# When VectorE takes sums of attention's weights ahead of mixing steps: a change to a scheduled BigBird and FNet kernel

## The chip, the cores and the metric

The kernel runs on one core of a Trainium2 chip. Its time is the device time of one launch in microseconds, a median of three runs. One further launch was recorded by the profiler; every stretch of time below is from that one.

## The reference

Two blocks follow each other. The first is attention with BigBird's block mask (4 batches, 8 heads, 768 positions, 64 channels a head); the second mixes by Fourier transforms, normalises, and runs a small network over the channels.

```python
scores = scale * np.matmul(q, k.transpose(0, 1, 3, 2))
scores = np.where(mask, scores, -1000000000.0)          # mask: blocks of 32
attn = np.exp(scores - np.max(scores, axis=-1, keepdims=True))
attn = attn / (np.sum(attn, axis=-1, keepdims=True) + 1e-09)
out = np.matmul(attn, v)
x = out.transpose(0, 2, 1, 3).reshape(B, S, H * D)      # 4 x 768 x 512
X = np.fft.fft(np.fft.fft(x, axis=1), axis=2)
u = x + np.real(X)
un = (u - mean(u)) / np.sqrt(var(u) + 1e-06)            # over the 512 channels
return u + np.maximum(un @ w_ch1, 0.0) @ w_ch2          # 512 -> 2048 -> 512
```

## The kernel before

Attention works on pairs of heads, n = 0 to 15, four pairs to a batch. A pair has twelve units, u = 12 n + w. A unit is 128 keys against one half (384) of the queries, for both heads: TensorE makes its scores s (L592, and L602 where the mask is added by TensorE too), ScalarE the exponential into e (L612; or L620 and then a multiplication by the mask on VectorE, L622), TensorE the product with the values (L666). The six units of a half are also added up, element by element, in an accumulator acc: that is `gather(u)`. A sum is one instruction on VectorE (L647, 128 x 768) or two on GpSimd (L652, 128 x 384 each). TensorE then adds acc over its partitions into sp (L751; `total`), VectorE puts sp away in sums (L719 for the first pair of a batch, L721 for the others), and the pair's outputs are transposed into xt (L689) and copied into x (L690). There are four buffers of e and two of acc; scores have two banks of PSUM, and sp and xt share one, ps_t.

Mixing runs beside the attention of the next batch. VectorE folds the rows of x by their symmetries (L802 to L846), TensorE transforms (zp, L874, and the transform across channels), VectorE adds the result to x (L944), takes means and variances (L955, L956, with GpSimd in L957 and L959), normalises (L969) and transposes blocks of 32 (L1031). Two groups of DMAs turn these: far from un, then unT from far (L1047). `right` (L1092) makes combinations of unT, `left` (L1105, L1106 for a fold; L1112) combinations of the first weights.

The first product of the channels is Strassen's (Winograd's form) on quads of tiles: `quad(p)` issues seven products on TensorE (L1138), adds them on VectorE (L1143) and applies relu on ScalarE (L1147). Inside it, `combine(j)` prepares the next quad's left operand on VectorE: j = 1 is the fold and is two instructions, j = 3 is one. The second product comes in one of two forms. Where `seven[p // 2]` is set, two quads make a round with seven products (yc, yz, yw, L1246); its right operands wt and of come from GpSimd (L1215, `round_right`), its left ones are prepared on GpSimd or VectorE (L1228, L1231), and ScalarE, VectorE and GpSimd add what comes out (L1251 to L1290). Elsewhere `channels` makes plain products y (L1305) that VectorE adds to x (L1310).

Everything is emitted by one planner in Python. It keeps a clock per engine (`when`); `busy(engine, cost, after)` moves one on. Each engine runs its instructions in the order in which the planner emitted them. The planner looks into four queues (`short`, `apart`, `late`, `due`) and puts steps of mixing between the steps of attention. `do_apart` takes one step of mixing; its kind is a letter: d, w and b are steps that are VectorE's, m and t need a bank of PSUM, "-" needs none. For kind b, the right combinations after the blocks have gone through DRAM, `state["back"]` is the time from which unT may be read, by an estimate, BACK[b], added to the clock.

For a unit whose mask TensorE adds, the sum is not emitted at once. The unit waits in `to_gather` and its sum is emitted when its products with the values are, or when a later step asks for it (`gather_to`). `gather` picks the engine by the planner's clocks:

```python
at = max(e_at[u], acc_at.get((n, half), 0.0))
sooner = max(when["DVE"], at) + 1.0 < max(when["POOL"], at) + 2.9
```

Of the kernel before, what the change touches and what calls it, by code (L numbers as in the profile page):

```python
# [104 lines left out]
def kernel(  # L105
# [93 lines left out]
    when = {"PE": 0.0, "ACT": 0.0, "DVE": 0.0, "POOL": 0.0}  # L199
    free = {"m": [0.0, 0.0], "t": [0.0]}  # L200

    def busy(engine, us, after=0.0):
        when[engine] = max(when[engine], after) + us
        return when[engine]
# [8 lines left out]
    def give(which, at):  # L213
        free[which[0]][which[1]] = at + HOP
# [3 lines left out]
    def room(i, shape, name, dtype=FP32):  # L218
        return big.tile(shape, dtype, tag=f"big{i}", name=name)
# [281 lines left out]
    by_pe, to_gather = set(), deque()  # L501
# [3 lines left out]
    s_at, e_at, e_free, oT_at, acc_at = {}, {}, {}, {}, {}  # L505
# [127 lines left out]
    def gather(u):  # L633


        n, w = divmod(u, UP)
        half, c = divmod(w, C)
        if c == 0:
            return
        if c == 1:  # L640
            acc_of[n, half] = acc_p.tile([P, 2, HS], FP32, tag="acc", name="acc")
        acc, e = acc_of[n, half], e_of[u]
        start = e_of[u - 1] if c == 1 else acc
        at = max(e_at[u], acc_at.get((n, half), 0.0))
        sooner = max(when["DVE"], at) + 1.0 < max(when["POOL"], at) + 2.9
        if u in by_pe and masks["by_pe"] and w < UP - SLOT and sooner:
            nc.vector.tensor_tensor(out=acc, in0=start, in1=e, op=ALU.add)  # L647
            acc_at[n, half] = busy("DVE", 1.0, at) + HOP
        else:

            for i in range(2):
                nc.gpsimd.tensor_add(out=acc[:, i, :], in0=start[:, i, :], in1=e[:, i, :])  # L652
            acc_at[n, half] = busy("POOL", 2.9, at) + HOP
        e_free[u] = acc_at[n, half]
# [344 lines left out]
    def mixer(b, xA, xB):  # L999
# [57 lines left out]
        def un_back():  # L1057
# [5 lines left out]
            fetch(1)  # L1063
            state["back"] = max(when["PE"], state["ready"]) + BACK[b] + late_by

# [51 lines left out]
        def quad(p):  # L1117

            g = p // 2 % 2 if last else 0
            if p % 2 == 0:  # L1120
                for i in range(2):
                    hs[g, i] = room((2, 0)[g] + i, [P, 4, HS], "h" + "AB"[i])
            if not last:
                if p % 2 == 0:
                    seven[p // 2] = state["alone"] and p // 2 < NF // 4 - 1
                elif seven[p // 2]:
                    state["drain"]()
                    sums_room()
                    for j in (1, 2, 4, 3):
                        round_right(p // 2, j)  # L1130
            l1, l2 = 2 * (p % 2), 2 * (p % 2) + 1
            h11, h12, h21, h22 = (hs[g, i][:, l, :] for l in (l1, l2) for i in range(2))
            a11, a12, s2, a22 = blocks(p)
            b11, b21, b22 = unT[0][:, K1, :], unT[0][:, K2, :], unT[1][:, K2, :]

            def product(to, a, c, after=0.0):
                for k in range(ND // 2):
                    nc.tensor.matmul(to, a[:, k, :], c[:, k, :], start=(k == 0),  # L1138
                                     stop=(k == ND // 2 - 1))
                return busy("PE", PRODUCT, after) + HOP  # L1140

            def plus(to, ps, a, at):
                tt(out=to, in0=ps, in1=a, op=ALU.add)  # L1143
                return busy("DVE", SUM, at) + HOP

            def relu(h, at):
                nc.scalar.activation(out=h, in_=h, func=ACT.Relu)  # L1147
                busy("ACT", RELU, at)

            def combine(j):  # L1150
                left(p + 1, j)
                busy("DVE", COMBINE)

            x, at = ps_m.tile([P, 512], FP32, tag="m", name="xp")[:, 0:HS], bank("m")
            z5, z7 = (ps_s.tile([P, 2, 512], FP32, tag="s", name=name)[:, 0, 0:HS]
                      for name in ("z5", "z7"))
            done = product(x, a11, b11)
            nc.scalar.copy(out=h11, in_=x)  # L1158
            p1 = busy("ACT", RELU, done) + HOP
            give(at, p1 - HOP)  # L1160
            y, at = ps_m.tile([P, 512], FP32, tag="m", name="yp")[:, 0:HS], bank("m")
            p2 = product(y, a12, b21)
            done = product(z7, s2, t[2])
            u2 = plus(h21, z7, h11, max(done, p1))
            c11 = plus(h11, y, h11, p2)
            relu(h11, c11)
            done = product(z5, s[1], t[1])
            plus(h12, z5, h21, done)
            combine(1)
            done = product(z7, s[3], t[3], u2)  # L1170
            u3 = plus(h21, z7, h21, done)
            c22 = plus(h22, z5, h21, done)
            z_at[0] = c22
            relu(h22, c22)
            combine(3)
            gap(0.0, 1.9)
            done = product(y, a22, t[4], c11)
            c21 = plus(h21, y, h21, done)
            give(at, c21 - HOP)
            relu(h21, c21)  # L1180
            gap(0.0, 1.9, "t")
            done = product(z7, s[4], b22, u3)
            z_at[1] = plus(h12, z7, h12, done)
            relu(h12, z_at[1])
            combine(4)
            if last:
                for j in ((1, 2), (3, 4))[p % 2]:
                    output_right(p // 4, j, p // 2 % 2)
            elif p % 2 == 1 and seven[p // 2]:
                state["soon"] = 0.4  # L1190

        seven = {}
# [161 lines left out]
        last = b == B - 1  # L1354
# [139 lines left out]
        for r in range(0 if last else NF // 4):  # L1494
# [9 lines left out]
    MOST, LEAST = 9.6, 2.5  # L1504
    COVER = 100.0
    AHEAD = 2.2
    BACK = 11.0, 13, 11.5
    HALF = 5.0
    ALONE = 3.0
    LEAVES = 13.0  # L1510
# [6 lines left out]
    state = {"paired": False, "total": None, "w": 0, "got": 0, "owed": 0.0, "ready": 0.0,  # L1517
             "back": 0.0, "place": None,
             "slot": 0, "alone": False, "drain": lambda: None}
# [5 lines left out]
    def behind(kind):  # L1525

        at = max(when["DVE"], state["ready"])
        return (0.25 if state["alone"] else 0.75) * (len(kind) - 1) if when["POOL"] > at else 0.0

    def do_apart():  # L1530
        kind, fn, pe, act, dve, _ = apart.popleft()
        if finished and kind[0] in "mt" and state["total"] in short:
            short.remove(state["total"])
            state["total"][2]()
        if kind[0] in "dwb":
            dve += behind(kind)
            state["ready"] = busy("DVE", dve, {"w": rstd_at[0] if rstd_at else 0.0,
                                               "b": state["back"]}.get(kind, state["ready"])) + HOP
            fn()
            return  # L1540
        done = state["ready"]
        if kind != "-":
            at = bank(kind[0])
            done = busy("PE", pe, done) + HOP
        fn()
        if act:
            done = busy("ACT", act, done) + HOP
        if dve:
            done = busy("DVE", dve, done) + HOP
        if kind != "-":  # L1550
            give(at, done - HOP)
        state["ready"] = done
# [8 lines left out]
    def gap(rest=0.0, ahead=None, kinds="tm", start=None):  # L1561

        used = "".join(k for k in "tm" if k not in kinds)
        if ahead is None:
            ahead = AHEAD if late else ALONE
        while apart:
            kind, fn, pe, act, dve, need = apart[0]
            if len(late) > need:
                break
            if kind[0] in "dwb":  # L1570
                dve += behind(kind)
                if kind in "wb" and (state["back"] if kind == "b" else rstd_at[0]) > max(
                        when["DVE"], when["PE"]) + 0.2:
                    break
                at = max(when["DVE"], state["ready"]) - when["PE"]
                if at + dve > rest + ahead if start is None else at > start:
                    break
            elif kind != "-":
                bank_at = max(min(free[k]) for k in kind)
                if (any(k in used for k in kind) or  # L1580
                        max(state["ready"], bank_at) > when["PE"] + 0.1):
                    break
                used += kind
            do_apart()
        for item in list(short):
            kind, ready, fn = item
            if kind not in used and max(ready, min(free[kind])) <= when["PE"] + 0.1:
                used += kind
                short.remove(item)
                fn()  # L1590
# [334 lines left out]
```

## Time and profile before

| | |
|---|---|
| median of three runs | 1026.3 us (1026.03 to 1027.15) |
| the profiled execution | 1026.41 us |
| its span | 1024.7 us |
| TensorE's granted clock | 0.999 |
| VectorE, ScalarE, GpSimd busy | 712.2, 372.4, 326.7 us |
| sums on VectorE, mean of one | L647: 0.95 us where GpSimd rests beside it |
| half sums on GpSimd (L652) | 160 that add to acc, mean 1050 ns; 42 that start one, mean 1126 ns |

The span runs from the first instruction to the last; the profiled execution's own time is a little longer than it. A row of the timeline gives start and duration in us, the engine, the line, the operation, what it writes and reads, the count of instructions joined in it, and in brackets how long the engine had been idle and what it waited for. PE is TensorE, DVE VectorE, ACT ScalarE, POOL GpSimd, and SPq the queue that issues DMAs.

### The profile page before, as it was taken

What the parts mean: (1) busy time and instruction counts of PE and PEld (TensorE: products, weight loads), DVE (VectorE), ACT (ScalarE), POOL (GpSimd) and SP (SyncE); (2) the same over time, 40 slices, a digit from 0 to 9 for tenths busy, and PEclk for the clock granted to TensorE, in tenths of its full rate; (3) what the DMA queues carried; (4) which work ended last, traced back from release to release, by engine and by line L of the source; (5) the groups of instructions that cost most, each with busy time, mean ns of one, the idle gap of its engine ahead of it and who ended that gap; (6) DMA issues with size and microseconds to landing.
All of it is one profiled execution on the core that took longest, in us unless ns stands there. A gap on an engine that the chain in (4) does not pass through costs nothing.

```text
span 1024.7 us, 13026 instructions
## 1 busy us (share of the span) xinstructions
PE 1006.3 (98%) x4512; PEld 559.2 (55%) x4512; DVE 712.2 (70%) x1295; ACT 372.4 (36%) x763; POOL 326.7 (32%) x363
## 2 busy tenths in 40 slices
PE   8999999999999999999999999999999999999997
PEld 4344345444767764444444775444444765578576
DVE  6899895977984766755578577765458565775664
ACT  6888765553222222433440322343220221210210
POOL 1000173657634315454553232356450231000000
PEclk9999999999999999999999999999999999999999
DMA  7768422291000008532230002831010001200001
GB/s 228 228 190 231 102 48 47 52 150 31 1 1 1 11 11 151 96 73 39 55 62 1 1 11 77 155 58 41 17 24 8 1 0 52 42 1 0 1 13 52
DMA packets 182308, 60.44 MB, mean 59 GB/s; under 512 B 163018, under 2 KB 173012, under 8 KB 182236
## 3 DMA queue, kind: packets, MB, share of 16 engines
q1 hardware_dynamic: 180844, 58.88, 25.7%
q10 hardware_dynamic: 1360, 0.66, 0.3%
q8 instruction: 37, 0.61, 0.3%
q14 instruction: 35, 0.29, 0.1%
q0 software_dynamic: 32, 0.01, 0.0%
HBM read 46.14 MB, written 15.73 MB: 60 GB/s over the span
## 4 chain that ended last, share of the span: by engine, by line
PE 82%; DVE 9%; ACT 2%; issue 2%; DMA 2%; POOL 1%; SPq 1%; ACTq 0%; DVEq 0%; POOLq 0%
PE z L1138 16%; PE y L1305 14%; PE s L592 10%; PE o L666 9%; PE yp L1138 7%; PE yy L1401 7%; PE xp L1138 4%; PE yz L1246 3%; PE zp L874 2%; PE yc L1246 2%; PE yw L1246 2%; PE sp L737 1%; ACT e L612 1%; DVE acc L647 1%; DVE x L944 1%
## 5 line engine op out<-in xcount | busy, mean ns | idle before, releaser
L652 POOL TENSOR_TENSOR acc<-acc,e 128x384 f32<-128x384 f32 x160 | 162.6, 1050 | 105.4 <-DVE e L622 85.8
L592 PE MATMUL s<-qT,kT 64*128 64x384 f32 x768 | 153.4, 514 | 6.1 <-ACT e L612 4.7
L666 PE MATMUL o<-e,vr 128*64 128x384 f32 x768 | 142.2, 497 | 0.0
L592 PEld LDWEIGHTS s<-qT,kT 64*128 64x128 f32 x768 | 63.9, 185 | 86.6 <-ACT e L612 24.1
L622 DVE TENSOR_TENSOR e<-s,mask 128x768 f32<-128x768 f32 x86 | 78.1, 950 | 47.2 <-ACT s L620 37.8
L620 ACT ACTIVATE s<-s 128x768 f32<-128x768 f32 x86 | 65.0, 792 | 108.3 <-PE s L592 108.2
L652 POOL TENSOR_TENSOR acc<-e 128x384 f32<-128x384 f32 x42 | 46.4, 1126 | 173.9 <-ACT e L612 119.9
L612 ACT ACTIVATE e<-s 128x768 f32<-128x768 f32 x106 | 80.9, 810 | 53.5 <-PE s L602 32.2
L1138 PE MATMUL z<-unT,t 128*128 128x384 f32 x256 | 93.3, 487 | 1.4 <-DVE hA L1143 1.4
L666 PEld LDWEIGHTS o<-e,vr 128*64 128x64 f32 x768 | 47.7, 136 | 69.8 <-issue 67.7
L1143 DVE TENSOR_TENSOR hA<-z,hA 128x384 f32<-128x384 f32 x64 | 35.6, 557 | 64.4 <-PE z L1138 64.3
L1259 POOL TENSOR_TENSOR x<-of,x 128x256 f32<-128x256 f32 x45 | 39.2, 875 | 124.9 <-ACT of L1251 61.7
L1147 ACT ACTIVATE hA<-hA 128x384 f32<-128x384 f32 x64 | 33.5, 523 | 121.9 <-DVE hA L1143 121.9
L1305 PE MATMUL y<-w_sb,hB 128*128 128x512 f32 x168 | 74.9, 596 | 0.0
L1305 PE MATMUL y<-w_sb,hA 128*128 128x512 f32 x168 | 74.6, 596 | 0.0
L1138 PEld LDWEIGHTS z<-unT,t 128*128 128x128 f32 x256 | 48.4, 190 | 36.4 <-DVE hA L1143 3.2
L1147 ACT ACTIVATE hB<-hB 128x384 f32<-128x384 f32 x64 | 33.5, 523 | 86.7 <-DVE hB L1143 86.7
L1310 DVE TENSOR_TENSOR x<-y,x 128x512 f32<-128x512 f32 x42 | 29.0, 690 | 48.9 <-PE y L1305 48.8
L1305 PEld LDWEIGHTS y<-w_sb,hA 128*128 128x128 f32 x168 | 31.3, 190 | 39.7 <-issue 38.1
L1305 PEld LDWEIGHTS y<-w_sb,hB 128*128 128x128 f32 x168 | 31.0, 190 | 38.2 <-issue 38.2
L1158 ACT COPY hA<-xp 128x384 f32<-128x384 f32 x32 | 15.3, 477 | 90.2 <-PE xp L1138 87.8
L1138 PE MATMUL z<-t,w_sb 128*128 128x384 f32 x128 | 46.7, 488 | 1.1 <-DVE t L1092 1.1
(237 smaller groups left out, 1728.3 us busy)
## 6 DMA issues: line engine op xcount, KB each, us to landing
wraw<-in_moe_w_ch_dram SPq DMA_DIRECT2D x32, 512.0 KB
vr<-in_v_dram SPq DMA_DIRECT2D x30, 192.0 KB
far<-un SPq DMA_DIRECT2D x18, 256.0 KB
unT<-far SPq DMA_DIRECT2D x24, 192.0 KB
qb<-in_q_dram SPq DMA_DIRECT2D x44, 96.0 KB
kb<-in_k_dram SPq DMA_DIRECT2D x44, 96.0 KB
falls<-x SPq DMA_DIRECT2D x9, 256.0 KB
out_dram<-x SPq DMA_DIRECT2D x18, 128.0 KB
```

The source lines that it names most:

```text
L592: nc.tensor.matmul(s[:, i, 0:HS], kT[rows, c * P:(c + 1) * P], qT[rows, queries], start=True, stop=u not in by_pe)
L612: nc.scalar.activation(out=e, in_=s[:, :, 0:HS], func=ACT.Exp, scale=scale)
L620: nc.scalar.activation(out=s[:, :, 0:HS], in_=s[:, :, 0:HS], func=ACT.Exp, scale=scale)
L622: nc.vector.tensor_tensor(out=e, in0=s[:, :, 0:HS], in1=m.broadcast_to([P, 2, HS]), op=ALU.mult)
L652: nc.gpsimd.tensor_add(out=acc[:, i, :], in0=start[:, i, :], in1=e[:, i, :])
L666: nc.tensor.matmul(o[D * i:D * i + D, :], vt[:, i, c, :], e[:, i, :], start=(c == 0), stop=(c == C - 1))
L1138: nc.tensor.matmul(to, a[:, k, :], c[:, k, :], start=(k == 0), stop=(k == ND // 2 - 1))
L1147: nc.scalar.activation(out=h, in_=h, func=ACT.Relu)
L1246: nc.tensor.matmul(to, a[:, k, :], c[:, k, :], start=start and k == 0, stop=k == 1, skip_group_check=True)
L1259: nc.gpsimd.tensor_add(out=to, in0=kept[i], in1=to)
L1305: nc.tensor.matmul(y, hs[0, half][:, l, m * P:(m + 1) * P], w2_sb[:, 4 * r + l, :], start=(l == 0), stop=(l == 3))
L1401: nc.tensor.matmul(ps, a[:, k, :], c[k // 2][:, k % 2, :] if isinstance(c, list) else c[:, k, :], start=(k == 0), stop=(k == 3))
```

## The change

Three edits. In `quad`, where the quad is the second of a round with seven products, the fold of the next quad's weights (`combine(1)`) is emitted behind two more additions, u3 and c22, and `combine(3)` behind c21. `BACK[1]`, the estimate for batch 1's blocks on their way back, goes from 13 to 14.2. In `do_apart`, ahead of a step of kind d, w or b, units that wait in `to_gather` are summed first if their exponentials are done by the time the step would start, and if GpSimd, on the planner's clock, would end the sum later than VectorE after that step.

```diff
@@ -1166,18 +1166,22 @@
             done = product(z5, s[1], t[1])
             plus(h12, z5, h21, done)
-            combine(1)
+            beside_wt = not last and p % 2 == 1 and seven[p // 2]
+            if not beside_wt:
+                combine(1)
             done = product(z7, s[3], t[3], u2)
             u3 = plus(h21, z7, h21, done)
             c22 = plus(h22, z5, h21, done)
             z_at[0] = c22
             relu(h22, c22)
-            combine(3)
+            combine(1 if beside_wt else 3)
             gap(0.0, 1.9)
             done = product(y, a22, t[4], c11)
             c21 = plus(h21, y, h21, done)
             give(at, c21 - HOP)
             relu(h21, c21)
+            if beside_wt:
+                combine(3)
             gap(0.0, 1.9, "t")
@@ -1504,7 +1508,7 @@
-    BACK = 11.0, 13, 11.5
+    BACK = 11.0, 14.2, 11.5
@@ -1533,6 +1537,12 @@
         if kind[0] in "dwb":
+            while to_gather:
+                u = to_gather[0]
+                at = max(when["DVE"], state["ready"])
+                if not (e_at[u] < at + 0.1 and max(when["POOL"], e_at[u]) + 2.9 > at + dve + 1.0):
+                    break
+                gather(to_gather.popleft())
             dve += behind(kind)
```

## The prediction

> **What bounds the kernel now.** I read the page's busy shares and clock first, then TensorE's waits, then the timeline around each place where the order changes. The profiled execution took 1026.41 us for a span of 1024.7, 1.7 us lying outside it; the median of the runs is 1026.3, so a sum made against 1026.41 stands for the median within 0.1 us.
>
> ```profile
> PE 1006.3 (98%) x4512; PEld 559.2 (55%) x4512; DVE 712.2 (70%) x1295; ACT 372.4 (36%) x763; POOL 326.7 (32%) x363
> PEclk9999999999999999999999999999999999999999
> ```
>
> TensorE is busy 1006.3 of 1024.7 us, at one clock from end to end, and the change gives it no matmul more or fewer. VectorE's 70% and GpSimd's 32% count only where one of their results comes last. So the question is which of TensorE's few idle stretches go and which are new.
>
> ```profile
> PE s L592 <- ACT e L612: 4.7, 12, 0.9
> ...
> PE z L1138 <- DVE hA L1143: 1.4, 3, 0.7
> PE z L1138 <- DVE t L1092: 1.1, 2, 1.0
> ```
>
> Columns: total us, times, longest. The first row is the one that the change can shorten: scores wait for a bank that an exponential empties, and that exponential (L612) waits for one of four buffers of weights, which a late sum holds. All twelve are 4.7 us, 0.5% of the time. That is the ceiling of any gain.
>
> **What is moved.** In the order of instructions, VectorE has four more sums of weights (L647) and GpSimd six fewer half sums (L652); all lie in batch 0's mixing, at two places (about 146 and 200 to 240 us). The channel sums of edit one move in three quads of batch 0 and two of later batches. The planner's clocks, changed by the moved sums, also exchange two of TensorE's steps near 392 us. BACK of 14.2 moves no instruction alone; beside the other edits it only keeps right's L1092 behind the channels' last L1310, as before. I cost it at nothing: without it two VectorE lines change places.
>
> **Place one, 146 to 165 us: what goes.**
>
> ```profile
> 157.23 0.92 PE L592 MATMUL s<-qT,kT 64*128 64x384 f32 x4 [0.27 <-ACT e L612]
> ...
> 163.60 0.92 PE L592 MATMUL s<-qT,kT 64*128 64x384 f32 x4 [0.86 <-ACT e L612]
> ...
> 162.73 0.81 ACT L612 ACTIVATE e<-s 128x768 f32<-128x768 f32 x1 [3.48 <-DVE acc L647]
> ...
> 161.69 0.95 DVE L647 TENSOR_TENSOR acc<-acc,e 128x768 f32<-128x768 f32 x1
> ```
>
> Start, duration, and in brackets the idle time before it with its releaser. The chain reads backwards: scores at 163.60 wait for the exponential at 162.73, which waits for the sum at 161.69, which stood behind the whole fold on VectorE. In the changed order units 61, 62 and 63 are summed ahead of the fold, 65 goes to GpSimd, and this sum no longer ends last. Both gaps go: 0.27 + 0.86 = 1.13 us won.
>
> **Place one: what is new.**
>
> ```profile
> 146.58 0.80 DVE L813 TENSOR_TENSOR e<-x 128x255 f32<-128x255 f32 x1
> ...
> 149.56 0.55 DVE L719 COPY sums<-sp 128x384 f32<-128x384 f32 x1
> ...
> 156.51 1.05 DVE L840 TENSOR_TENSOR e<-e 128x128 f32<-128x128 f32 x1
> ...
> 149.00 2.63 POOL L652 TENSOR_TENSOR acc<-e 128x384 f32<-128x384 f32 x2 [0.77 <-PE sp L751]
> ...
> 152.31 0.55 PE L689 MATMUL xt<-ident,oT 128*128 128x128 f32 x3
> ...
> 160.32 0.59 PE L874 MATMUL zp<-cs_sb,e 128*128 128x192 f32 x2
> ...
> 207.51 0.93 DVE L647 TENSOR_TENSOR acc<-e 128x768 f32<-128x768 f32 x1
> ```
>
> Unit 61's sum starts a new accumulator, of which there are two; on GpSimd it began at 149.00, released by the totals L751 that read the old one. Now this wait stands at the head of VectorE, which had begun the fold at 146.58: some 2.4 us of VectorE idle, then three sums of 0.93 (alone, the last row), until 149.0 + 2.8 = 151.8. Behind it stand L813 to L815 and then L719. They took 146.58 to 148.78, 2.2 us, mostly beside a GpSimd sum; with no GpSimd beside them they would take about 0.9 (an estimate: 2.2 scaled as L821 below, 0.48 against 1.22). L719 therefore ends between 151.8 + 0.9 + 0.55 = 153.2 and 151.8 + 2.2 + 0.55 = 154.5, and not at 150.1. L719 empties the one bank of ps_t, and the transposition xt at 152.31 needs that bank: TensorE stalls there 0.9 to 2.2 us. I take 1.5, about the middle, since GpSimd's next sum can start no earlier than 151.8, when these steps do, and lies beside the later ones.
>
> The fold itself starts 5.2 us later. Its first output ended at 156.51 + 1.05 = 157.56, 10.98 after L813's start, and one sum of 0.9 within leaves it: 151.8 + 10.1 = 161.9. zp reads it at 160.32 before; delayed by 1.5 and advanced by 0.27 it comes at 161.55. The stall there is 0.35 if all of it counts, 0 if the fold runs less beside GpSimd; I take 0.1. Without the stall of xt it would be 1.5 more, so one of the two stalls comes whichever is first. Place one: 1.5 + 0.1 - 1.13 = +0.5, from 0.9 - 1.13 = -0.2 to 2.2 + 0.5 - 1.13 = +1.6.
>
> ```profile
> 150.71 1.22 DVE L821 SCALAR_TENSOR_TENSOR sa<-sa,not_first 128x257 f32<-128x257 f32 x1
> 151.85 1.22 DVE L821 SCALAR_TENSOR_TENSOR sa<-sa,ident 128x257 f32<-128x257 f32 x1
> ...
> 290.78 0.48 DVE L821 SCALAR_TENSOR_TENSOR e<-sa,not_first,e 128x257 f32<-128x257 f32 x1
> ...
> 125.97 1.95 POOL L652 TENSOR_TENSOR acc<-acc,e 128x384 f32<-128x384 f32 x2 [2.27 <-ACT e L612]
> ```
>
> The two engines slow each other: a fold step takes 1.22 beside a GpSimd sum (starts 1.14 apart) and 0.48 alone; a pair of half sums 1.95 alone and 2.63 beside the fold.
> The Trainium skill's page "SBUF — State Buffer", section "SBUF: two separate sides", holds that VectorE operations with two SBUF inputs and GpSimd ones take the shared port pair as an exclusive lock for a whole instruction, the other blocking fully. By that rule a step and a half sum would alternate at 0.48 + 0.97 = 1.45 us, four such steps would end the fold 1.2 us later, and the sum below would be +2.4 instead of +1.2; the trace has 1.14, so sharing is milder than that.
>
> **Place two, 200 to 249 us.**
>
> ```profile
> 209.42 1.62 PE L592 MATMUL s<-qT,kT 64*128 64x384 f32 x8 [0.66 <-ACT e L612]
> ...
> 236.06 0.92 PE L592 MATMUL s<-qT,kT 64*128 64x384 f32 x4 [0.59 <-ACT e L612]
> ...
> 229.82 1.13 DVE L1092 TENSOR_TENSOR t<-unT 128x768 f32<-128x768 f32 x1 [0.36 <-DMA unT<-far]
> ...
> 237.81 1.74 DVE L647 TENSOR_TENSOR acc<-acc,e 128x768 f32<-128x768 f32 x1 [1.84 <-POOL acc L652]
> ...
> 242.91 0.56 DVE L1143 TENSOR_TENSOR hA<-z,hA 128x384 f32<-128x384 f32 x1 [1.90 <-PE z L1138]
> ```
>
> The sum at 207.51 moves up some 5 us, ahead of normalising steps; unit 99's on GpSimd, which the scores at 236.06 wait for, goes to VectorE, earlier. Both gaps go: 0.66 + 0.59 = 1.25. In exchange the transpositions L1031 come behind three or four sums of 0.93: 2.8 to 3.7 us later, and with them the DMAs that write far and fetch unT from it, on SP's queue now behind four fetches of q, which wait for nothing but their buffers. The first L1092, which waited for unT to 229.82, comes 3 to 4 us later. VectorE's slack up to 242.91 is 1.84 + 1.90, and the sum of 1.74 there goes to GpSimd: 5.5 us, more than the delay. But TensorE reads the L1092 sums before 242.91, so not all of the slack may serve; back come 0 to 1.8, and I take 0.1. What is late next is L1092. Place two: -1.15, from -1.25 to +0.5.
>
> **The exchange near 392 us.**
>
> ```profile
> 392.48 1.56 PE L592 MATMUL s<-qT,kT 64*128 64x384 f32 x8
> ...
> 394.35 3.60 PE L1305 MATMUL y<-w_sb,hB 128*128 128x512 f32 x8
> ...
> 400.81 0.85 PE L751 MATMUL sp<-acc,pick 128*32 128x384 f32 x8
> ...
> 396.40 3.86 POOL L652 TENSOR_TENSOR acc<-acc,e 128x384 f32<-128x384 f32 x4 [4.53 <-DVE e L622]
> ```
>
> ```profile
> L622 DVE TENSOR_TENSOR e<-s,mask 128x768 f32<-128x768 f32 x86 | 78.1, 950 | 47.2 <-ACT s L620 37.8
> L620 ACT ACTIVATE s<-s 128x768 f32<-128x768 f32 x86 | 65.0, 792 | 108.3 <-PE s L592 108.2
> ```
>
> The scores at 392.48 go through exponential, mask (L622) and two sums on GpSimd, which end at 400.26, just before the totals at 400.81. The 3.5 us of y ran under that. In the changed order y stands ahead of the scores, so they start at 392.48 + 3.5 = 396.0; the mask, which waited for VectorE's channel steps, no longer does, and the first product comes after half the scores, one exponential and one mask, 0.78 + 0.79 + 0.95 = 2.5, 2.8 with the hops between (an estimate), instead of 396.40 - 392.48 = 3.9: at 398.8; GpSimd ends at 402.7. The first half of the totals (0.42 us) needs none of it; the second waits from 401.2 to 402.7. Cost 1.5, from 1.0 (mask earlier) to 2.0; I take 1.4. Nothing behind it waits for another engine for long enough to take it back.
>
> **The quads' channel sums.**
>
> ```profile
> 257.00 0.42 DVE L1106 TENSOR_TENSOR w_sb<-t,w_sb 128x256 f32<-128x256 f32 x1
> 257.36 0.56 DVE L1143 TENSOR_TENSOR hA<-z,hA 128x384 f32<-128x384 f32 x1
> 257.95 0.56 DVE L1143 TENSOR_TENSOR hB<-z,hA 128x384 f32<-128x384 f32 x1
> 258.43 0.42 DVE L1112 TENSOR_TENSOR t<-w_sb 128x256 f32<-128x256 f32 x1
> 258.76 0.55 DVE L1143 TENSOR_TENSOR hA<-yp,hA 128x384 f32<-128x384 f32 x1
> ...
> 259.35 0.52 ACT L1147 ACTIVATE hA<-hA 128x384 f32<-128x384 f32 x1 [0.28 <-DVE hA L1143]
> ...
> 259.74 1.03 PE L1246 MATMUL yc<-w_sb,hA 128*128 128x256 f32 x4
> ```
>
> Now u3 at 257.36 follows L1105 and L1106 without a gap and TensorE does not wait for it, so moving them saves nothing. Moved behind c22, they replace one L1112 ahead of c21: 2 x 0.42 - 0.42 = +0.42 us. The relu that follows ends at 259.87 and yc reads it directly, within 0.1 us, so TensorE waits up to 0.4. Three quads of batch 0 have this form: 0 to 1.2; I take 0.5, since waits for GpSimd shortly after absorb part. In the two later quads another product lies between: 0.
>
> **Sum.** +0.5 - 1.15 + 1.4 + 0.5 = +1.2 (rounded): 1026.4 + 1.2 = 1027.6 us.
>
> **Rivals.** (1) The gaps go and nothing is given back: VectorE gets through 61 to 63 soon enough for xt and zp, and the totals at 400.8 are covered. Then 1.13 + 1.25 = 2.4 less: 1024.0. For it: the gaps have clear releasers. Against it: the wait of unit 61 at VectorE's head. Chance 0.15. (2) Slower: VectorE's head of line. If L719 comes at the upper end (xt +2.2), zp +0.35 behind it, the exchange costs 2.0 and the quads 1.0, while the gaps of 2.4 are won, that is 2.2 + 0.35 + 2.0 + 1.0 - 2.4 = +3.2: 1029.6. It decides once L719 ends later than 152.31 + 1.13 = 153.4, when xt's stall outweighs the gaps won. Chance 0.25. (3) TensorE's work simply slides and the change does not do what it says: gaps move to the next buffer, 1026.4. For it: TensorE at 98%. Chance 0.1. The sum as worked keeps 0.5.
>
> **How the numbers follow.** A difference of 0.2%, 2.05 us, is about what a measurement tells from none; "faster" is below 1024.25, "slower" above 1028.35. Faster: most of rival 1 and a little of the forecast's lower side, 0.14. Slower: rival 2 and a fifth of the forecast, 0.34. The rest, 0.52, is within. The range leaves out most of rival 1 and the far end of rival 2: 1025.0 to 1029.8.
>
> **What would show it.** Right: no gaps at places one's 163.6 and two's 209.4 and 236.1; a wait of xt on VectorE near 152; a wait of sp L751 on GpSimd near 401; yc waiting 0.1 to 0.4 us for a relu near 260. Wrong: xt without a wait, or L719 ahead of 152.3; a wait of z for L1092 near 240 of over 0.5 us, which place two costs at almost nothing; a time below 1025.

## The result, and the profile after

The changed kernel takes 1028.73 us (median of 11 runs, 1027.83 to 1032.44) against 1026.69 before (11 runs beside it). The ratio is 1.0024, 95% interval 1.0015 to 1.0033: it is slower by 2.0 us where 1.2 was forecast. The sign and the range were right, the size was not: by the prediction's own bounds 1028.73 lies above 1028.35 and so in "slower", to which it gave 0.34, and not in "within", to which it gave 0.52. TensorE's waits in the changed kernel, in the columns that were shown of before:

```profile
PE xt L689 <- DVE sums L719: 2.7, 1, 2.7
PE warm L326 <- POOL ident masks.py:199: 2.6, 1, 2.6
PE s L592 <- ACT e L612: 2.5, 8, 0.5
PE xt L689 <- ACT oT L677: 1.9, 2, 1.4
PE s L592 <- DVE e L622: 1.6, 2, 0.8
PE z L1138 <- DVE t L1092: 1.1, 2, 0.9
```

The scores' wait for exponentials fell from 4.7 to 2.5 us: that is the gain. Two waits of xt and one of the scores for a masked product are new.

The cost of each place is read by setting TensorE's matmuls of both traces beside each other and taking the difference of their starts. At 148 us the changed kernel is 0.55 us behind, all of it from the first 10 us, where the order is the same. After that it moves as follows:

| stretch (times of before) | steps of the difference, us | sum | forecast |
|---|---|---|---|
| place one, to 164 us | +2.8 at xt, -0.44, -1.13 | +1.2 | +0.5 |
| place two, to 248 us | -0.24, -0.73, -0.35, +1.38 at xt, -0.14, -0.76, -0.94 | -1.8 | -1.15 |
| quads, to 343 us | +0.20, -0.13, +0.22, +0.14 | +0.4 | +0.5 |
| exchange, to 402 us | -2.60 + 3.55, +0.22, +0.78 | +1.95 | +1.4 |

The sum is +1.8 us, and the spans differ by 2.3 with the start's 0.55. The start is not counted as the change's: in the traces of the other runs it differs from before's too, by 0.1 to 1.1 us.

Place one, in the timeline of the changed kernel:

```profile
149.62 0.96 DVE L647 TENSOR_TENSOR acc<-e 128x768 f32<-128x768 f32 x1 [2.24 <-PE sp L751]
150.68 2.02 DVE L647 TENSOR_TENSOR acc<-acc,e 128x768 f32<-128x768 f32 x2
152.62 0.41 DVE L813 TENSOR_TENSOR e<-x 128x255 f32<-128x255 f32 x1
152.95 0.97 DVE L814 COPY e<-x 128x2 f32<-128x2 f32 x1
153.96 1.17 DVE L815 SCALAR_TENSOR_TENSOR e<-e,flip,sa 128x257 f32<-128x257 f32 x1
155.05 0.54 DVE L719 COPY sums<-sp 128x384 f32<-128x384 f32 x1
...
152.85 4.80 POOL L652 TENSOR_TENSOR acc<-acc,e 128x384 f32<-128x384 f32 x4 [4.07 <-DVE acc L647]
...
155.65 0.55 PE L689 MATMUL xt<-ident,oT 128*128 128x128 f32 x3 [2.73 <-DVE sums L719]
```

Unit 61's sum waits at VectorE's head for 2.24 us, the sums end at 152.70, and of the three steps ahead of L719 the last two run beside GpSimd's next sums, which begin at 152.85. xt waits until L719 has emptied the bank.

Place two: who holds ScalarE ahead of the second xt.

```profile
212.80 3.24 SPq L1032 DMA_DIRECT2D far<-un  x2
216.13 2.92 SPq L1047 DMA_DIRECT2D unT<-far  x3
219.15 3.36 SPq L236 DMA_DIRECT2D qb<-in_q_dram  x4
...
225.67 0.84 ACT L549 ACTIVATE qT<-qb 128x768 f32<-128x768 f32 x1 [1.93 <-DMA qb<-in_q_dram]
...
226.51 0.46 ACT L677 COPY oT<-o 128x384 f32<-128x384 f32 x1
...
227.02 0.55 PE L689 MATMUL xt<-ident,oT 128*128 128x128 f32 x3 [1.42 <-ACT oT L677]
```

The four fetches of q are issued at 219.15, not at 214.53 as before: on SP they stand behind two writes of far, the second of which now waits for a later L1031 (it is issued at 215.71, where the last write ahead of q was issued at 213.46 before), and behind the three fetches of unT that follow these writes. So q lands later, ScalarE waits 1.93 us for it with the copy of o behind, and xt waits 1.42.

### The profile page after: what moved, and what is told of

Same layout as the page of the kernel before. It is cut to its first block, busy times and chain, and to the rows that moved or that the text cites. A ratio compares the mean times of both kernels' runs of the same rounds, so it can differ in the third digit from the quotient of the medians.

```text
span 1027.0 us, 13021 instructions
## 1 busy us (share of the span) xinstructions
PE 1007.2 (98%) x4512; PEld 560.0 (55%) x4512; DVE 711.5 (69%) x1298; ACT 373.1 (36%) x763; POOL 320.6 (31%) x357
## 4 chain that ended last, share of the span: by engine, by line
PE 87%; DVE 6%; ACT 2%; DMA 2%; issue 2%; SPq 1%; ACTq 0%; DVEq 0%
PE z L1138 15%; PE y L1309 13%; PE s L592 12%; PE o L666 11%; PE yp L1138 7%; PE yy L1405 7%; PE xp L1138 4%; PE yz L1250 3%; PE zp L874 2%; PE yc L1250 2%; PE yw L1250 2%; PE s L602 1%; PE sp L737 1%; PE sp L751 1%; PE xt L689 1%
## 5 line engine op out<-in xcount | busy, mean ns | idle before, releaser
L622 DVE TENSOR_TENSOR e<-s,mask 128x768 f32<-128x768 f32 x86 | 78.3, 950 | 48.3 <-ACT s L620 38.9
L652 POOL TENSOR_TENSOR acc<-e 128x384 f32<-128x384 f32 x38 | 40.3, 1082 | 172.2 <-ACT e L612 120.8
L1143 DVE TENSOR_TENSOR hA<-z,hA 128x384 f32<-128x384 f32 x64 | 35.6, 557 | 65.1 <-PE z L1138 65.0
```

Of the source, the lines that this page charges most:

```text
L622: nc.vector.tensor_tensor(out=e, in0=s[:, :, 0:HS], in1=m.broadcast_to([P, 2, HS]), op=ALU.mult)
```

## The experiments

Each was timed in five rounds beside the kernel before (11 runs of each, 10 for `best` and 5 for `stall_more`; the medians of before are 1026.46 to 1026.56).

**The quads' edit alone.** The three lines in `quad`, nothing else.

> Only the quads' edit (the fold of the next weights behind two additions). Theory: it delays the relu that yc reads by some 0.2 us in three quads, +0.4 us in all, so the time is within 1 us of before. Rival: the quads' sums are what costs, and this edit alone shows most of the 2 us. Second rival: it does what it is for (VectorE free of the sums beside GpSimd's), and the time falls by 0.5 to 1 us.

1027.24 us, ratio 1.0007 (0.9998 to 1.0016). Its trace has +0.24, -0.14, +0.23 and +0.14 at the three quads, +0.47 in all; the rest is the start. At the first of them yc takes 1.34 us, where it took 1.03:

```profile
259.97 1.34 PE L1250 MATMUL yc<-w_sb,hA 128*128 128x256 f32 x4
```

The edit costs what the theory said, and the waits that it was to shorten did not change: scores 4.7, z 1.4 and 1.1 us, as before. Against no change the timing alone does not decide.

**The other two edits alone.**

> Without the quads' edit: the sums ahead of mixing steps and the estimate of 14.2. Theory: these carry nearly all of the loss, +1.6 to +2.0 us: place one +1.2, place two -1.8, the exchanged steps near 400 us +1.95. Rival: the edits add up only together, and this one is within 0.5 us of before.

1027.58 us, ratio 1.0012 (1.0003 to 1.0021): +1.0, less than expected in time. In its trace TensorE goes +1.2 by place one, -1.6 by place two and +1.8 at the exchange, +1.4 in all. The rival, that the edits add up only together, is out.

**Place one alone.**

```diff
-                if not (e_at[u] < at + 0.1 and ...
+                if u // UP > 5 or not (e_at[u] < at + 0.1 and ...
```

> Sums go ahead of steps only in the first place (units 61 to 63, at about 150 us); nothing else changes. Theory: xt waits 2.7 us for L719, two gaps of 1.1 us go, the remainder stays: +1.2 us. Rival: the steps of the following quads take the delay back, and the time is that of before.

1028.32 us, ratio 1.0019 (1.001 to 1.0029). The trace shows +2.70 at xt, then -0.44 and -1.13, and -0.26 at 201 us (the changed kernel has that step too; the table books it under place two). Nothing more of it is taken back. In time this place alone comes near the whole change; the median is half a microsecond above the profiled execution (1027.79), and why is not shown.

**Place two alone**, with the exchange that comes of it (`u // UP < 6 or not`).

> Sums go ahead of steps only in the second place (200 to 240 us), with the exchange of y and scores near 400 us that comes of it. Theory: -1.8 us by 248 us and +1.95 at the exchange, so +0.15 us in all, equal to before; the trace shows xt waiting 1.4 us at 225 for a copy behind ScalarE's qT. Rival: place two alone is the gain of the edit, and the time falls by 1.5 us or more.

1027.2 us, ratio 1.0007 (0.9998 to 1.0016). The trace gives -1.2 by 248 us, less than expected, and +1.8 at the exchange. The gain is there, and is lost 150 us later. The medians of the three parts taken alone (+0.7, +1.8, +0.6) add up to 3.1 us where the whole is 2.0; each is uncertain by about 0.9, so the parts are read from the traces.

**The sums behind L719.** As place one, but the three sums are emitted when `total(4)` has put its result away.

```diff
+            def add():
+                nc.vector.tensor_tensor(out=acc, in0=start, in1=e, op=ALU.add)
+            if u in (61, 62, 63):
+                held.append(add)
+            else:
+                add()
...
         give(at, busy("DVE", 0.6, busy("PE", 0.7, acc_at[n, 1]) + HOP))
+        while n == 4 and held:
+            held.pop(0)()
```

> As the run place_one, but VectorE takes the three sums behind L719, not ahead of L813. Theory (the stall of xt is L719 standing behind the sums): xt no longer waits 2.7 us, both gaps stay gone, so place one gives about -1.3 us instead of +1.2: 2.5 us below place_one. Rival (the sums' own time delays the fold, whatever their place): zp then waits for the fold by about 1.5 us, and the time is that of before or above.

1026.57 us, ratio 1.0001 (0.9992 to 1.001), 1.75 us below place one. The timeline:

```profile
149.57 0.56 DVE L726 COPY sums<-sp 128x384 f32<-128x384 f32 x1 [0.37 <-PE sp L758]
150.05 0.95 DVE L650 TENSOR_TENSOR acc<-e 128x768 f32<-128x768 f32 x1
...
161.03 0.28 DVE L848 TENSOR_TENSOR e<-e 128x128 f32<-128x128 f32 x1
...
161.37 0.59 PE L883 MATMUL zp<-cs_sb,e 128*128 128x192 f32 x2 [1.11 <-DVE e L848]
```

(L726 is L719, L650 is L647, L830, L848 and L883 are L821, L839 and L874 of before.) xt no longer waits: that L719 stood behind the sums is shown to be the cause of the 2.7 us. But zp now waits 1.11 us for the fold, which the stall of xt had covered. Of the two stalls one comes whichever is first, as the prediction put it, and the place gains 0.6 us in the trace (-0.44 + 1.07 - 1.02 - 0.2; place one, counted alike, loses 0.9) where theory said 1.3. Both expectations were half right.

**Place two with y behind the scores.** The planner's loop skips the step at the slot concerned; TensorE's order is then that of before.

```diff
-        while not more and rest():
+        while not more and rest() and sl != 52:
```

> As the run place_two, but the y step stays behind the scores, as before. Theory: the exchange is a loss of 1.8 to 1.95 us by itself, and without it the time is 1.3 to 1.8 us below before, and 1.8 below place_two. Rival: something else ahead of the totals takes the gain back, and the time stays within 0.5 us of place_two.

1025.55 us, ratio 0.9992 (0.9983 to 1.0001), 1.65 below place two. It is 0.9 below before, where 1.3 to 1.8 was expected, and the interval just reaches no change. In its trace nothing moves near 400 us. The exchange is a loss by itself.

**And the fetches of q on ScalarE.**

```diff
-                nc.sync.dma_start(
+                (nc.scalar if (n, a) == (9, 0) else nc.sync).dma_start(
```

> As place_two_kept, with the four fetches of q for pair 9 issued by ScalarE and not by SP. Theory: on SP they stand behind two writes of far that wait for a late L1031, so qT, the copy of o and xt come late; freed of that queue xt's wait of 1.4 us at 225 goes, and the time falls by up to 1.4 us more, to 2.7 to 3.2 below before. Rival: the four issues on ScalarE delay exponentials by as much, or z's wait at 248 takes the gain back, and nothing is left of it.

1025.07 us, ratio 0.9987 (0.9978 to 0.9996). Waits in its trace:

```profile
PE s L592 <- ACT e L612: 3.7, 11, 0.9
...
PE xt L689 <- ACT oT L677: 0.5, 1, 0.5
```

The 1.4 us wait of xt is gone, so the queue was its cause. The median falls by 0.5 us, though, not by 1.4. The traces of this run and the one before it gain 2.3 and 1.3 us at place two, so 1.0 of the 1.4 is there. The four issues hold ScalarE for 2.88 us, and the exponential behind them starts after 2.56 us in which ScalarE computes nothing; scores then wait 0.2 us for it. That is a part of the rival:

```profile
213.48 2.88 ACTq L236 DMA_DIRECT2D qb<-in_q_dram  x4
216.46 1.51 ACT L612 ACTIVATE e<-s 128x768 f32<-128x768 f32 x2 [2.56 <-DMA qb<-in_q_dram]
```

A further 0.2 us is lost at 603 us, and the time that lies outside the span is 2.0 us (the median of these runs), where it is 1.7 in the run before. Why these two grow is not shown.

**The whole change with y behind the scores.**

> The whole change, with the y step behind the scores as before. Theory: 1.9 us below the changed kernel, so within 0.5 us of before: +0.4 of the quads, +1.2 and -1.8 of the two places. Rival: the exchange costs the changed kernel less, and it stays 1 us or more above before.

1027.88 us, ratio 1.0018 (1.0009 to 1.0028). Three runs lie at 1026.6 to 1026.7, as the theory had it, four at 1027.6 to 1028.1, and four at 1029.6 to 1030.3. The profiled run took 1030.24, and its trace shows why (stretches, then PE's busy time and instructions, its weights', the other engines', and behind them the granted clock and two columns on DMAs):

```profile
140.00:150.00 10.00, 10.00 (x66) 3.99 (x68) 7.36 (x7) 6.81 (x12) 6.40 (x5) 1.00 0.38 80
150.00:158.00 8.00, 5.27 (x27) 2.56 (x29) 7.76 (x9) 3.31 (x10) 4.80 (x4) 0.83 0.31 51
158.00:164.00 6.00, 6.00 (x28) 2.23 (x26) 5.79 (x11) 1.99 (x3) 2.13 (x2) 0.66 0.01 1
164.00:172.00 8.00, 8.00 (x51) 4.80 (x49) 4.01 (x6) 4.77 (x10) 1.45 (x2) 1.00 0.00 0
```

xt's wait is 2.73 us, as in the changed kernel. But now the clock falls, and the matmuls up to 162.1 us take nearly twice as long:

```profile
156.74 2.93 PE L592 MATMUL s<-qT,kT 64*128 64x384 f32 x8
...
162.58 1.56 PE L592 MATMUL s<-qT,kT 64*128 64x384 f32 x8
```

That costs 2.9 us more (the difference from before goes from 3.6 at xt to 6.5). Apart from it the steps are those of the table with the exchange at 0. In stretches of 0.2 us the granted clock is 1.00 up to about 155.3 us, 0.50 from there to about 162.1 and 1.00 again: it falls within the wait, before xt starts at 155.91.

**The stall made longer.** As place one, with L719's copy made three times (`for _ in range(3 if key == 1 else 1)`).

> As place_one, with L719's copy of 0.55 us made three times, so that xt waits 1.1 us more: 3.8 us. Theory (a longer wait lets the clock fall more often): the profile shows granted clock below 1 behind 150 us, and the median rises by well over 1.1 us, to 3 to 4 us above place_one. Rival: the clock has nothing to do with the length of the wait, and the time rises by 1.1 us alone.

1031.0 us (1030.57 to 1032.09), ratio 1.004 (1.0026 to 1.0054): 2.7 us above place one for 1.3 us of further stall.

```profile
157.22 0.87 PE L689 MATMUL xt<-ident,oT 128*128 128x128 f32 x3 [4.01 <-DVE sums L720]
158.02 2.93 PE L592 MATMUL s<-qT,kT 64*128 64x384 f32 x8
```

```profile
158.00:164.00 6.00, 6.00 (x25) 2.57 (x26) 5.76 (x13) 2.47 (x4) 1.10 (x2) 0.65 0.02 4
```

The clock fell here too (0.65 in the second fence, the stretch behind the stall). It is 0.50 from about 155.3 to 162.1 us, as in `after_kept`; the longer wait takes up more of that stretch, so the matmuls lose 2.3 us behind it and not 2.9. The rise is above the rival's, which leaves out the clock, but below the 3 to 4 that the theory named. The profiled execution is the longest of the five (mean clock 0.996, the others 0.998). Whether some of place one's own runs paid for the clock already is open: its times spread from 1027.28 to 1029.15, with mean clocks of 0.997 to 1.000 that do not go with the times.

**The changed kernel again.**

> The changed kernel once more, for the spread of its times. Theory (xt's wait of 2.7 us lets TensorE's clock fall to half for some 6 us in part of the executions, which adds 3 us): most runs at 1027.8 to 1029.3, and a few 3 us above them, with none in between by more than 1.5 us. Rival: the high ones were a chance of one chip, and all runs lie within 1.5 us.

1028.5 us, ratio 1.0021 (1.0012 to 1.003). Nine runs lie at 1028.0 to 1029.2 and two at 1030.0 and 1030.2; in the first eleven two lay at 1032.1 and 1032.4. So there are high runs each time, but not at one distance of 3 us. The mean granted clock of each run goes with its time: 0.996 for the two at 1032, 0.997 for the two at 1030, 0.998 to 0.999 for the other eighteen; in `after_kept` 0.995 to 0.996 for the four highest, 0.997 for the four in the middle and 0.998 to 1.000 for the three lowest. A loss of 0.003 over 1028 us is 3 us. That is the size of the excess, so the clock accounts for the high runs; that it falls at xt's wait in each of them is argued from the one trace of `after_kept`.

**What can be kept of it.** Both places, the sums behind L719, y behind the scores, the fetches on ScalarE and the quads as before.

> Both places and the fetches of q on ScalarE, the three sums behind L719, the y step behind the scores, and the quads as before. Theory: the parts add up, 0 to -0.5 us of place one and -1.4 to -2.0 of place two: 1.4 to 2.5 us below before. Rival: place one's later fold makes z wait at place two, and the two together give no more than place two alone.

1024.67 us, ratio 0.998 (0.997 to 0.9989): 1.9 us below before and 3.8 below the changed kernel beside it, the fastest of all. In its trace TensorE gains 0.5 us by place one and 2.2 by place two, so the parts add up and the rival is out there; in time it lies 0.4 below place two alone, which is within the uncertainty. Its longest wait besides the start is now one of a microsecond:

```profile
PE s L592 <- ACT e L612: 3.1, 9, 0.7
...
PE zp L883 <- DVE e L848: 1.1, 1, 1.1
```

## Why the prediction was right, and where its sizes were off

- **Ceiling and sign.** The argument from TensorE's 98% held: the scores' waits for exponentials fell by 2.2 of their 4.7 us. The ceiling was drawn too low, though, as z's waits for L1143, which it left out, fell by 0.7. The new waits are 2.7 and 1.4 at xt, 0.8 at the scores and 0.8 within the totals.
- **The order.** VectorE has three sums more than before (22 L647 against 19), not four, which fits GpSimd's six fewer half sums. No run takes the 14.2 away from the other edits, so this term, put at nothing, is untested.
- **Place one, the stall of xt.** The mechanism was the forecast one; the term was mis-sized, 2.73 against 1.5 taken and 2.2 at the upper end. The three sums took 3.1 us, not 2.8, and the steps ahead of L719 2.4, not 0.9 to 2.2. L813 took 0.41 instead of 0.80 and L814 0.97, as before, but L815, which had run alone in 0.49, now ran beside GpSimd's next sums and took 1.17. So 2.2 was no upper bound. L719 ended 1.1 us later than the upper end of the forecast, 0.5 of it the later start of this execution.
- **Place one, zp.** No stall, as 0.1 said, since xt's was the longer. The sentence that one of the two comes was shown by `behind_total`.
- **Place two.** The gaps went, and one more than counted: z's 0.67 at 247.68. The step that failed is the one on SP's queue: "four fetches of q, which wait for nothing but their buffers" was read for what stands behind them. What stands ahead of them, two writes of far, one of them waiting for a late L1031, and the fetches of unT, was not costed. It is 1.42 us. L1092, named as the next to be late, starts 6 us later, not 3 to 4, and holds nothing up.
- **The exchange.** Mechanism right, +1.95 against 1.4 (upper end 2.0); 1.84 of it comes from 390 us on. GpSimd ended at 403.15, and as this execution was 0.53 us late at 390, that is the 402.7 of the forecast. What was mis-sized is where the wait counts from: before, the totals' matmuls start together, the last at 400.83 and not at 401.2; now the last starts at 403.21, and 403.21 - 400.83 - 0.53 = 1.85. A wait that was not seen comes ahead of it, 0.77 us of the scores behind xt for a bank that the mask multiplication (L622) holds; it adds nothing, since what it delays waits for GpSimd in any case:

```profile
399.25 1.78 PE L592 MATMUL s<-qT,kT 64*128 64x384 f32 x8 [0.77 <-DVE e L622]
402.40 1.65 PE L751 MATMUL sp<-acc,pick 128*32 128x384 f32 x8
...
399.27 3.88 POOL L652 TENSOR_TENSOR acc<-acc,e 128x384 f32<-128x384 f32 x4 [6.92 <-DVE e L622]
```

The totals take 1.65 instead of 0.85: the wait within them.
- **The quads.** 0.4 against 0.5, with the place and the cause as forecast.
- **The sum.** The traces have +1.8 against +1.2, from errors of both signs: +0.7 at place one, -0.6 at place two, +0.55 at the exchange, -0.1 in the quads. Within place two the 1.4 of xt, which was not costed, is made up by gains that were not counted, z's above all. That the time lies as near as it does is in part luck.
- **Rivals.** The four gaps of the first are gone (2.4 us), but not without the stalls. What the second was to be decided by came true: L719 ended at 155.6, later than 153.4. Its 1029.6 was not reached, as the quads cost 0.4 and not 1.0, zp did not wait, and place two gained more. The third is out.
- **The rule of the exclusive lock, which the prediction cites.** In `behind_total` the four L821 that run beside GpSimd's sums start 1.15, 1.15 and 1.26 us apart, near the 1.14 of before and not the 1.45 of the rule; once GpSimd rests, one takes 0.48 again:

```profile
153.90 1.23 DVE L830 SCALAR_TENSOR_TENSOR e<-sa,not_first,e 128x257 f32<-128x257 f32 x1
155.05 1.23 DVE L830 SCALAR_TENSOR_TENSOR sa<-sa,not_first 128x257 f32<-128x257 f32 x1
156.20 1.22 DVE L830 SCALAR_TENSOR_TENSOR sa<-sa,ident 128x257 f32<-128x257 f32 x1
157.46 1.10 DVE L830 SCALAR_TENSOR_TENSOR sa<-sa,flip 128x257 f32<-128x257 f32 x1
...
161.56 0.48 DVE L830 SCALAR_TENSOR_TENSOR sd<-sd,not_first 128x257 f32<-128x257 f32 x1
```

## What to carry to other kernels

A sum that an engine would make anyway is free only where nothing that another engine needs stands behind it: before moving work ahead, list what its queue holds next, and ask which bank each of those instructions empties. The same goes for the DMA queue on both sides, what is behind a moved issue and what is ahead of it. And where a planner keeps clocks, a moved step can exchange others hundreds of microseconds away; read the order of the whole program before costing the edit.

## What was not expected of the hardware

A TensorE pause of 2.73 us left the granted clock at 1.00 in four traces (the changed kernel twice, place one, the two edits); in the fifth, `after_kept`, the clock was 0.50 from about 155.3 to 162.1 us, which cost 2.9 us. A pause of 4.01 us had the same stretch at 0.50 and cost 2.3 us beyond itself. So the price of the stall of 2.73 us is the stall, or about twice that. The Trainium skill, on the page "TensorE: Matmul & The Clock Gate", section "Part 1: The HAM clock gate (the "warmup" mystery)", has the clock at half after at least one idle window of about 3.4 us, in a window that runs freely. That it does not happen every time agrees; that 2.73 us can be enough is the measurement, and in `after_kept` the clock fell 2.1 us after the last matmul ended (153.2 us by the profile).
